# Attention scores by query blocks of one head, two heads in the two row halves of TensorE, in an attention, routing and expert kernel

## Chip, cores and metric

The kernel runs on one core of a Trainium2 chip. The metric is the device time of one launch in microseconds (us). A core has five engines that run side by side and meet only through semaphores: TensorE (PE: matrix products and transposes; its weight loads are shown as PEld), VectorE (DVE), ScalarE (ACT), GpSimd (POOL) and SyncE (SP, which issues DMAs). SBUF is the working memory, of 128 partitions; PSUM holds what PE writes, in 8 banks of 512 fp32 columns. PE's clock has two levels, 2.4 and 1.2 GHz; a granted clock of 1.0 is the upper one.

## The reference

Three stages, each fed by the one before. Only the first is touched by the change.

```python
B, H, S, D = 4, 8, 576, 64                      # attention
scores = scale * np.matmul(q, k.transpose(0, 1, 3, 2))
scores = np.where(causal, -1e9, scores)
scores = scores - scores.max(-1, keepdims=True)
a = np.exp(scores); a /= a.sum(-1, keepdims=True) + 1e-09
local = np.matmul(a, v)
q_p = phi(q)                                     # where(q > 0, q, exp(q) - 1) + 1
mem_out = (q_p @ M_prev) / ((q_p * z_prev).sum(-1) + 1e-6)
x = g * mem_out + (1 - g) * local                # g = sigmoid(beta), per head
# then: a top-1 mixture of 8 experts over 2304 tokens, and a gated layer 512 -> 1536 -> 512
```

## The kernel before

`attention_moe_gated` builds three stages: `Attention.run` (with `Routing` planned into it), `Experts.experts`, `Experts.gated`. The change lies in `Attention` and in one piece of `Routing.logits`.

**Tiles.** Two heads make a pair `pi`, 16 pairs in all; two pairs make a load group `gi`. `turn` transposes q, k and phi(q) of a pair on PE, so that one head lies on partitions 0 to 63 and the other on 64 to 127. The scores are made with fp32r products, which keep fewer bits: q and k are split into a high and a low part (`q_part`, `k_part`; ACT writes the high one, DVE subtracts it for the low one), and a score is the sum of three products. A score block (`scores`, L345) has 64 query rows of each head, 128 rows in all. Its weights `qz` are block diagonal: the 64 rows of the one head meet zeros in the half of the other, so that one product with 128 contraction rows gives both heads. A pair has nine such blocks of 64 to 576 key columns.

**Softmax.** `masked` (DVE, L365) adds the causal mask and takes the row minimum of the negated scores out of PSUM; `exp` (ACT, L375) makes the exponents and their row sums; `turn_probs` (PE, L410) transposes them in pieces of 128 columns; `keep_probs` (ACT or DVE, L283 or L285) copies them into `pt`, with a copy of its own for a last piece of 64 rows. `out_part` (PE, L440) multiplies with v, the two heads in the two column halves of the array; `mem_part` (L426) adds the memory term.

**The factors.** After the nine blocks of a pair, `recip` (DVE, L384 and L385) takes the reciprocals of the 128x9 sums. `spread` (L390, POOL or DVE) multiplies them into a 128x576 diagonal pattern `dg`, `fan` (PE, L398) spreads `dg` over the partitions with two fp32 products of 288 columns, `fan_copy` keeps them as `rb`, and `out_scale` (DVE, L450) multiplies the output with `rb`.

**POOL.** Beside this POOL makes phi(q), once per load group: `phi_sum` (L258, L260, L262, L264) is four operations on 128x1152 values that follow each other, below called a phi chain; then DVE reduces (`phi_norm`) and POOL scales (`phi_scale`, L276).

**What sets the order.** `Plan` is a list scheduler that runs when the program is built. Each step has a rank, a cost for each engine that may take it, what it needs and what buffer it takes; `order` picks the step that can start first by these costs, and all engines' queues are written in that order. At run time each engine works strictly through its queue. Buffers are pools: three PSUM banks for scores, three for transposes, two for outputs.

Of the kernel before, what the change touches and what calls it, by code (L numbers as in the profile page):

```python
# [30 lines left out]
SMB = 4  # L31
# [9 lines left out]
ORDER = (8, 0, 7, 1, 6, 2, 5, 3, 4)  # L41
# [83 lines left out]
class Attention:  # L125


    def __init__(self, ctx, tc, q, k, v, M_prev, z_prev, beta, ident, routing, high):
# [7 lines left out]
        self.ps_s = ctx.enter_context(tc.tile_pool(name="ps_s", bufs=3, space=PSUM))  # L136
        self.ps_t = ctx.enter_context(tc.tile_pool(name="ps_t", bufs=3, space=PSUM))
        self.ps_o = ctx.enter_context(tc.tile_pool(name="ps_o", bufs=2, space=PSUM))
        self.constants(beta)

    def constants(self, beta):
# [26 lines left out]
        self.iog = cp.tile([P, H // 2], F32, name="iog")  # L168
        for j in range(2):
            r = slice(j * 64, (j + 1) * 64)  # L170
            nc.vector.tensor_copy(self.iog[r], og[r].rearrange("p (a j) -> p a j", j=2)[:, :, j])
        nc.vector.reciprocal(self.iog, self.iog)

        self.rows = cp.tile([P, 64], F32, name="rows64")
        nc.vector.tensor_tensor(self.rows, self.ident[:, 0:64], self.ident[:, 64:128], ALU.add)
        self.same = cp.tile([P, P], F32, name="same")
        nc.gpsimd.memset(self.same, 0.0)
        for j in range(2):
            r = slice(j * 64, (j + 1) * 64)
            nc.gpsimd.memset(self.same[r, r], 1.0)  # L180
# [151 lines left out]

    @staticmethod
    def spans(t):
        n = 64 * (t + 1)
        return [(0, n)] if n <= 512 else [(0, 288), (288, 576)]

    def scores(self, u, si):
        nc, (pi, n_) = self.nc, divmod(u, NQ)
        t = ORDER[n_]  # L340
        k0, k1 = self.spans(t)[si]
        z, kz = self.qz[pi % 2], self.kz[pi]
        self.Sp[u, si] = Sp = self.ps_s.tile([P, 512], F32, name="Sp", tag="Sp")
        for p_, (a, c) in enumerate(((0, 0), (0, 1), (1, 0))):
            nc.tensor.matmul(  # L345
                Sp[:, 0 : k1 - k0], lhsT=z[:, a, t, :], rhs=kz[:, c, k0:k1], start=(p_ == 0), stop=(p_ == 2)
            )

    def masked(self, u, si):

        pi, n_ = divmod(u, NQ)
        t = ORDER[n_]
        n = 64 * (t + 1)
        if n_ == 0:
            self.sums[pi] = self.w2.tile([P, NQ], F32, name="sums", tag="sums")
        if si == 0:

            o = 0 if n_ % 2 == 0 else self.two[u // NQ, n_ // 2][1]
            if n_ % 2 == 0:
                self.two[pi, n_ // 2] = self.sp.tile([P, 640], F32, name="Sm", tag="Sm", bufs=SMB), n  # L360
            self.Sm[u] = self.two[pi, n_ // 2][0][:, o : o + n]
            self.mx[u] = self.sp.tile([P, 2], F32, name="mx", tag="mx")
        k0, k1 = self.spans(t)[si]
        mx = self.mx[u]
        self.nc.vector.tensor_tensor_reduce(  # L365
            out=self.Sm[u][:, k0:k1], in0=self.Sp[u, si][:, 0 : k1 - k0],
            in1=self.mask[:, 512 - 64 * t + k0 : 512 - 64 * t + k1],
            scale=-0.125, scalar=3.0e38 if si == 0 else mx[:, 0:1],
            op0=ALU.add, op1=ALU.min, accum_out=mx[:, si : si + 1],
        )  # L370

    def exp(self, u):
        pi, n_ = divmod(u, NQ)
        si = len(self.spans(ORDER[n_])) - 1
        self.nc.scalar.activation(  # L375
            self.Sm[u], self.Sm[u], AF.Exp, scale=-1.0, bias=self.mx[u][:, si : si + 1],
            accum_out=self.sums[pi][:, ORDER[n_] : ORDER[n_] + 1],
        )

    def recip(self, pi):  # L380

        nc, hp = self.nc, pi % (H // 2)
        self.rc[pi] = rc = self.sp.tile([P, NQ], F32, name="rc", tag="rc", bufs=2)
        nc.vector.tensor_scalar(rc, self.sums[pi], 1e-9, self.iog[:, hp : hp + 1], ALU.add, ALU.mult)  # L384
        nc.vector.reciprocal(rc, rc)  # L385

    def spread(self, eng, pi):

        self.dg[pi] = dg = self.w2.tile([P, NQ, 64], F32, name="dg", tag="dg", bufs=1)
        (self.nc.vector if eng == "DV" else self.nc.gpsimd).tensor_tensor(  # L390
            dg, self.rows[:, None, :].to_broadcast([P, NQ, 64]), self.rc[pi][:, :, None].to_broadcast([P, NQ, 64]), ALU.mult
        )

    def fan(self, pi, bk):

        self.TR[pi, bk] = T = self.ps_t.tile([P, 512], F32, name="T", tag="T")
        dg = self.dg[pi].rearrange("p t r -> p (t r)")
        self.nc.tensor.matmul(T[:, :288], lhsT=self.same, rhs=dg[:, bk * 288 : (bk + 1) * 288], start=True, stop=True)  # L398
# [6 lines left out]
    def turn_probs(self, u, chunks):
        nc, t = self.nc, ORDER[u % NQ]
        self.TP[u, chunks[0]] = T = self.ps_t.tile([P, 512], F32, name="T", tag="T")
        for n, i in enumerate(chunks):
            kr = min(128, 64 * (t + 1) - 128 * i)
            nc.tensor.transpose(T[:kr, n * 128 : (n + 1) * 128], self.Sm[u][:, i * 128 : i * 128 + kr], self.ident)  # L410

    def keep_probs(self, eng, u, c0, c1, first):

        pi, t = u // NQ, ORDER[u % NQ]
        kr = min(128, 64 * (t + 1) - 128 * c0)
# [1269 lines left out]
```

## Time and profile before

| | us |
|---|---|
| timed runs | 1131.64, 1125.78, 1129.64; median 1129.64 |
| profiled execution, its own time | 1123.5 |
| its span (first to last instruction) | 1121.7, mean granted clock 0.97 |
| PE / PEld / DVE / ACT / POOL busy over the span | 1037.1 / 900.6 / 545.5 / 466.5 / 293.8 |
| attention: first score product to the copy of the last logits | 9.71 to 299.0 |

Attention with its routing is about the first quarter of the span; the experts and the gated layer, whose rows are nearly all PE, follow and are not touched. A busy PE is not a PE at its peak, since the recorded length of a product holds its latency; what a product costs in a stream is the distance to the start of the next one. Where rows are merged (x3), the first start and the count are shown, and the start of the next row tells how long they held the engine.

### The profile page before, as it was taken

Reading aid. Unit: us, or ns where it says so; the run is one execution under the profiler, and the core shown is the slowest. Engines: PE = TensorE matmul, PEld = TensorE weight load, DVE = VectorE, ACT = ScalarE, POOL = GpSimd, SP = SyncE. Lnnn points to the kernel's source line nnn. Section 1 sums busy time; section 2 is a strip of 40 time slices with the busy share of each in tenths; the row PEclk is TensorE's granted clock in tenths of the full one; section 3 lists DMA queues with packets and bytes.
Section 4 is the critical chain, followed back from the end, with each engine's and each line's share of the span. In section 5 each row is a group of like instructions: output and inputs, shape, how many; then the busy total and the mean of one; then the engine's idle time right before and its main releaser. Section 6 shows DMA issues by size and latency. Waiting matters only on the chain. (4 is left out here: it accounts for less than half of the span.)

```text
span 1121.7 us, 16871 instructions
## 1 busy us (share of the span) xinstructions
PE 1037.1 (92%) x6133; PEld 900.6 (80%) x6133; DVE 545.5 (49%) x1232; ACT 466.5 (42%) x1074; POOL 293.8 (26%) x287
## 2 busy tenths in 40 slices
PE   6998998999869799979987679999999999999997
PEld 5766776777559689968976579999899999999996
DVE  6888867767585153227225699941212111121112
ACT  5875776777545252126214365521212211221211
POOL 7667245333265152025114300000110100100101
PEclk9999999999979999989998989999999999999999
DMA  5646433322268264128224466500010100100000
GB/s 119 140 103 175 83 85 85 97 61 58 66 196 291 75 210 159 38 72 280 87 62 137 141 188 197 177 12 1 29 57 1 47 10 1 58 1 1 29 1 29
DMA packets 111899, 102.50 MB, mean 91 GB/s; under 512 B 69520, under 2 KB 86928, under 8 KB 111760
## 3 DMA queue, kind: packets, MB, share of 16 engines
q1 hardware_dynamic: 107888, 88.18, 26.8%
q0 software_dynamic: 3872, 12.62, 3.7%
q8 instruction: 69, 1.13, 0.5%
q14 instruction: 70, 0.57, 0.2%
HBM read 84.49 MB, written 16.28 MB: 90 GB/s over the span
## 5 line engine op out<-in xcount | busy, mean ns | idle before, releaser
L1482 DVE TENSOR_TENSOR G<-G,pT 128x384 f32<-128x384 f32 (+1 forms) x74 | 40.1, 543 | 248.7 <-PE pT L1468 248.5
L1514 POOL DMA_INDIRECT out_dram<-o,rows x18 | 17.5, 971 | 462.7 <-ACT o L1510 213.5
L345 PE MATMUL Sp<-kz,qz 128*128 128x288 f32 (+8 forms) x480 | 100.3, 340 | 7.6 <-DVE mx L365 7.6
L1489 ACT ACTIVATE Gh<-G 128x384 fp32r<-128x384 f32 (+1 forms) x74 | 38.2, 516 | 162.3 <-DVE G L1482 162.1
L1478 ACT ACTIVATE G<-pH 128x384 f32<-128x384 f32 x72 | 35.4, 491 | 129.9 <-PE pH L1468 129.8
L345 PEld LDWEIGHTS Sp<-kz,qz 128*128 128x128 f32 x480 | 73.9, 197 | 17.0 <-DVE mx L365 9.5
L375 ACT ACTIVATE Sm<-Sm,mx 128x576 f32<-128x576 f32 (+2 forms) x144 | 79.8, 557 | 16.3 <-DVE mx L365 16.0
L1102 POOL TENSOR_TENSOR W<-raw,W 128x1024 fp32r<-128x1024 f32 x23 | 60.5, 2632 | 76.5 <-ACT W L1097 76.4
L365 DVE CUSTOM_DVE_ANT_0 Sm<-Sp,mask 128x288 f32<-128x288 f32 (+2 forms) x144 | 63.4, 450 | 18.8 <-PE Sp L345 12.4
L1499 PE MATMUL pX<-W,Gh 128*128 128x512 f32 x220 | 68.9, 394 | 0.0
L1097 ACT ACTIVATE W<-raw 128x1024 fp32r<-128x1024 f32 x60 | 61.7, 1054 | 16.9 <-DMA y_dram<-y 8.4
L283 ACT ACTIVATE pt<-T 64x128 f32<-64x128 f32 (+4 forms) x159 | 53.6, 368 | 31.9 <-PE T L410 28.2
L410 PE MATMUL T<-ident,Sm 128*128 128x128 f32 (+1 forms) x400 | 61.6, 281 | 5.0 <-ACT pt L283 3.4
L440 PE MATMUL O<-pt,vn 128*64 128x288 f32 (+4 forms) x512 | 59.5, 352 | 0.0
L1102 DVE TENSOR_TENSOR W<-raw,W 128x1024 fp32r<-128x1024 f32 x37 | 55.0, 1497 | 7.1 <-ACT W L1097 7.1
L1487 DVE TENSOR_TENSOR Gl<-G,Gh 128x384 fp32r<-128x384 f32 (+1 forms) x74 | 40.4, 546 | 33.9 <-ACT Gh L1489 33.9
L410 PEld LDWEIGHTS T<-ident,Sm 128*128 128x128 f32 (+1 forms) x400 | 43.3, 136 | 16.5 <-ACT pt L283 5.1
L1233 PE MATMUL pH<-W,xh 128*128 128x512 f32 x80 | 28.4, 501 | 28.3 <-issue 28.1
L1468 PE MATMUL pT<-xh,W 128*128 128x384 f32 x264 | 52.5, 342 | 0.0
L1468 PE MATMUL pT<-yh,W 128*128 128x384 f32 x264 | 51.3, 336 | 0.0
L440 PEld LDWEIGHTS O<-pt,vn 128*64 128x64 f32 (+1 forms) x512 | 30.4, 137 | 23.6 <-issue 11.2
L1468 PE MATMUL pH<-yh,W 128*128 128x384 f32 x240 | 46.9, 337 | 1.4 <-DVE xl L1457 1.4
(325 smaller groups left out, 2459.5 us busy)
## 6 DMA issues: line engine op xcount, KB each, us to landing
raw<-in_moe_w_dram SPq DMA_DIRECT2D x60, 512.0 KB, 4.9
raw<-in_moe_w_gate_dram SPq DMA_DIRECT2D x12, 512.0 KB, 4.3
raw<-in_moe_w_val_dram SPq DMA_DIRECT2D x12, 512.0 KB, 3.7
raw<-in_moe_w_out_dram SPq DMA_DIRECT2D x12, 512.0 KB, 3.3
y_dram<-y SPq DMA_DIRECT2D x9, 513.0 KB, 3.1
qn<-in_q_dram SPq DMA_DIRECT2D x32, 128.0 KB, 2.8
kn<-in_k_dram SPq DMA_DIRECT2D x32, 128.0 KB, 2.7
zf<-in_z_prev_dram SPq DMA_DIRECT2D x32, 128.0 KB, 5.8
```

Of the source, the lines that this page charges most:

```text
L283: self.nc.scalar.activation(out, in_, AF.Copy)
L345: nc.tensor.matmul(Sp[:, 0 : k1 - k0], lhsT=z[:, a, t, :], rhs=kz[:, c, k0:k1], start=(p_ == 0), stop=(p_ == 2))
L365: self.nc.vector.tensor_tensor_reduce(out=self.Sm[u][:, k0:k1], in0=self.Sp[u, si][:, 0 : k1 - k0], in1=self.mask[:, 512 - 64 * t + k0 : 5 ...
L375: self.nc.scalar.activation(self.Sm[u], self.Sm[u], AF.Exp, scale=-1.0, bias=self.mx[u][:, si : si + 1], accum_out=self.sums[pi][:, ORDER[ ...
L410: nc.tensor.transpose(T[:kr, n * 128 : (n + 1) * 128], self.Sm[u][:, i * 128 : i * 128 + kr], self.ident)
L440: nc.tensor.matmul(O[j * 64 : (j + 1) * 64, q0 - q0b : 288], lhsT=self.G[gi, "v"][:kr, i, 2 * l + j, :], rhs=PT[:kr, j, i, q0:q1], start=( ...
L1097: self.nc.scalar.activation(hi, t, AF.Copy)
L1102: eng.tensor_tensor(lo, t, hi.bitcast(F32), ALU.subtract)
L1468: nc.tensor.matmul(t, lhsT=w[:, k * P : (k + 1) * P], rhs=x[:, k, :], start=(m == k == 0), stop=(m == 2 and k == 3),)
L1482: nc.vector.tensor_tensor(t, t, p, ALU.mult)
L1487: nc.vector.tensor_tensor(l, t, hi.bitcast(F32), ALU.subtract)
L1499: nc.tensor.matmul(po[g][jj], lhsT=a[:, ts], rhs=w, start=(f == 0 and m == 0), stop=(f == NF - 1 and m == 2), skip_group_check=True,)
```

## The change

**Scores.** The blocks of 64 query rows of both heads become blocks of 128 query rows of one head (128 x 128, 256, 384 or 512 keys). The contraction is then 64 rows: head 0 uses the upper half of PE's rows and head 1 the lower, as tiles of 64x128, and their products alternate in the queue, into two PSUM banks of one buffer. Rows 512 to 575 stay as they were, one block-diagonal block of 576 columns (`z8`). There are still nine mask steps with ten instructions, nine exponents and 25 transposes in a pair, with 3136 instead of 2880 score columns; the copies out of the transposes are 10 instead of 13. `q_part` works on all 128 partitions at once, with four small pieces for `z8`.

**Factors.** `recip` becomes four DVE instructions on 128x9 values, which end in a high and a low part side by side (128x18). PE transposes these (`rc_turn`), a copy keeps them (18x128), and `fan` spreads them with six fp32r products against a constant choice matrix `pick` (made once on POOL). `spread` is gone.

**Buffers.** Scores: two buffers of two banks; transposes and outputs share four banks. Output halves are 384 and 192 columns instead of twice 288.

```diff
-ORDER = (8, 0, 7, 1, 6, 2, 5, 3, 4)
+ORDER = (3, 0, 2, 1, 4)
...
-        self.ps_s = ctx.enter_context(tc.tile_pool(name="ps_s", bufs=3, space=PSUM))
-        self.ps_t = ctx.enter_context(tc.tile_pool(name="ps_t", bufs=3, space=PSUM))
-        self.ps_o = ctx.enter_context(tc.tile_pool(name="ps_o", bufs=2, space=PSUM))
+        self.ps_s = ctx.enter_context(tc.tile_pool(name="ps_s", bufs=2, space=PSUM))
+        self.ps_t = ctx.enter_context(tc.tile_pool(name="ps_t", bufs=4, space=PSUM))
...
+    PARTS = ((0, 0), (0, 1), (1, 0))
...
+    def scores(self, pi, c):
+        nc, kz = self.nc, self.kz[pi]
+        self.Sp[pi, c] = Sp = self.ps_s.tile([P, 2, 512], F32, name="Sp", tag="Sp")
+        if c < 4:
+            n, q = 128 * (c + 1), self.qT[pi % 2]
+            for p_, (a, k) in enumerate(self.PARTS):
+                for j in range(2):
+                    r = slice(j * 64, j * 64 + 64)
+                    nc.tensor.matmul(
+                        Sp[:, j, 0:n], lhsT=q[r, a, c * 128 : (c + 1) * 128], rhs=kz[r, k, 0:n],
+                        start=(p_ == 0), stop=(p_ == 2), skip_group_check=True,
+                    )
+        else:
+            for i, (k0, k1) in enumerate(self.spans(8)):
+                for p_, (a, k) in enumerate(self.PARTS):
+                    nc.tensor.matmul(
+                        Sp[:, i, 0 : k1 - k0], lhsT=self.z8[pi % 2][:, a, :], rhs=kz[:, k, k0:k1],
+                        start=(p_ == 0), stop=(p_ == 2),
+                    )
...
-        self.rc[pi] = rc = self.sp.tile([P, NQ], F32, name="rc", tag="rc", bufs=2)
-        nc.vector.tensor_scalar(rc, self.sums[pi], 1e-9, self.iog[:, hp : hp + 1], ALU.add, ALU.mult)
-        nc.vector.reciprocal(rc, rc)
-
-    def spread(self, eng, pi):
-
-        self.dg[pi] = dg = self.w2.tile([P, NQ, 64], F32, name="dg", tag="dg", bufs=1)
-        (self.nc.vector if eng == "DV" else self.nc.gpsimd).tensor_tensor(
-            dg, self.rows[:, None, :].to_broadcast([P, NQ, 64]), self.rc[pi][:, :, None].to_broadcast([P, NQ, 64]), ALU.mult
-        )
+        self.rc[pi] = rc = self.sp.tile([P, 2 * NQ], F32, name="rc", tag="rc", bufs=2)
+        t = self.sp.tile([P, NQ], F32, name="rs", tag="rs", bufs=2)
+        nc.vector.scalar_tensor_tensor(t, self.sums[pi], 1e-9, self.iog[:, hp], ALU.add, ALU.mult)
+        nc.vector.reciprocal(t, t)
+        nc.vector.tensor_copy(rc.bitcast(F32R)[:, 0:NQ], t)
+        nc.vector.tensor_tensor(rc[:, NQ:], t, rc[:, 0:NQ], ALU.subtract)
+
+    def rc_turn(self, pi):
+        self.TR[pi] = T = self.ps_t.tile([P, 512], F32, name="T", tag="T")
+        self.nc.tensor.transpose(T[0 : 2 * NQ, 0:P], self.rc[pi], self.ident)
...
-        dg = self.dg[pi].rearrange("p t r -> p (t r)")
-        self.nc.tensor.matmul(T[:, :288], lhsT=self.same, rhs=dg[:, bk * 288 : (bk + 1) * 288], start=True, stop=True)
+        r = self.rT[pi]
+        for n in range(3) if bk == 0 else (3,):
+            o = (n - 3 * bk) * P
+            self.nc.tensor.matmul(T[:, o : o + P], lhsT=self.pick[:, n], rhs=r, start=True, stop=True, skip_group_check=True)
+        for j in range(2 * bk):
+            self.nc.tensor.matmul(
+                T[:, P : P + 64], lhsT=self.pick[:, 4 + j], rhs=r[:, j * 64 : (j + 1) * 64],
+                start=(j == 0), stop=(j == 1), skip_group_check=True,
+            )
```

On PE, a stretch of the second pair before: each row `L345` is three products with 128 contraction rows, and a block of 64 rows of both heads.

```order
L345 MATMUL Sp<-kz,qz_107 128x512 x3
L295 MATMUL T<-ident,qn 128x128 x4
L299 MATMUL T<-ident,qn 128x64
L410 MATMUL T<-ident,Sm 128x128 x2
L345 MATMUL Sp<-kz,qz_107 128x128 x3
L345 MATMUL Sp<-kz,qz_107 128x448 x3
L345 MATMUL Sp<-kz,qz_107 128x192 x3
```

The same place now: `L373` is the score product of a half (six: three parts for each of two heads), `L455` the transposes of exponents, `L311` and `L315` those of q and k, `L380` the last block.

```order
L373 MATMUL Sp<-kz,qT_105 128x512 x6
L455 MATMUL T<-ident,Sm 128x128 x7
L373 MATMUL Sp<-kz,qT_105 128x128 x6
L311 MATMUL T<-ident,qn 128x128 x4
L315 MATMUL T<-ident,qn 128x64
L455 MATMUL T<-ident,Sm 64x128
L455 MATMUL T<-ident,Sm 128x128 x4
L373 MATMUL Sp<-kz,qT_105 128x384 x6
L373 MATMUL Sp<-kz,qT_105 128x256 x6
```

The score groups are fewer and twice as long in count, and each now stands as 64x128 tiles between transposes that use the whole array.

On PE, where the factors of the last pair are spread, before (`L398` is `fan`, `L440` is `out_part`, `L426` is `mem_part`):

```order
L398 MATMUL T<-dg,same 128x288
L440 MATMUL O<-pt_144,vn 64x288 x2
L440 MATMUL O<-pt_144,vn 64x160 x2
L440 MATMUL O<-pt_144,vn 64x32 x2
L398 MATMUL T<-dg,same 128x288
L426 MATMUL O<-phT,MB 128x288
```

and now (`L427` is `rc_turn`, `L439` and `L441` are `fan`, `L489` is `out_part`):

```order
L427 MATMUL T<-ident,rc 18x128
L489 MATMUL O<-pt_147,vn 64x384 x2
L439 MATMUL T<-rT,pick 128x128 x4
L441 MATMUL T<-rT,pick 128x64 x2
L489 MATMUL O<-pt_147,vn 64x256 x2
L489 MATMUL O<-pt_147,vn 64x128 x2
L475 MATMUL O<-phT,MB 128x384
```

A transposition stands ahead, and the two fp32 products of 288 columns have become six small ones.

On DVE, the end of the first pair before (`L384` and `L385` are `recip`; `L310` the low part of q, `L365` masks):

```order
L384 TENSOR_SCALAR rc<-sums,iog 128x9
L385 RECIPROCAL rc<-rc 128x9
L310 TENSOR_TENSOR qz_106<-T,qz_106 64x6x64 x2
L310 TENSOR_TENSOR qz_106<-T,qz_106 64x3x64 x2
L365 ISA Sm,mx<-Sp,mask 128x128
```

and now, at the end of the second pair (`L402` masks, `L346` the low part of k, `L301` copies):

```order
L402 ISA Sm,mx<-Sp,mask 128x128
L402 ISA mx 128x1
L346 TENSOR_TENSOR kz<-T,kz 128x192
L420 SCALAR_TENSOR_TENSOR rs<-sums,iog 128x9
L421 RECIPROCAL rs<-rs 128x9
L422 CAST rc<-rs 128x9
L423 TENSOR_TENSOR rc<-rs,rc 128x9
L301 COPY pt_147<-T 128x2x128
L402 ISA Sm,mx<-Sp,mask 128x384
```

Four instructions that read and write SBUF alone stand where two stood, and masks and copies queue behind them.

## Rows read from the trace of the kernel before

**Rows 1.** Windows: stretch, length, busy us of PE, PEld, DVE, ACT, POOL; clock; DMA.
```profile
10.00:130.00 120.00, 108.40 (x723) 82.91 (x722) 98.37 (x284) 83.82 (x256) 77.19 (x54) 0.97 0.57 132
130.00:290.00 160.00, 156.06 (x1124) 118.75 (x1122) 111.97 (x373) 117.02 (x358) 62.24 (x48) 0.99 0.29 71
```

**Rows 2.** Timeline of PE (start, length): score products (L345) and what starts next.
```profile
135.25 0.39 PE L345 MATMUL Sp<-kz,qz 128*128 128x512 f32 x1
135.48 0.27 PE L410 MATMUL T<-ident,Sm 128*128 128x128 f32 x1
...
136.09 0.39 PE L345 MATMUL Sp<-kz,qz 128*128 128x128 f32 x2
136.31 0.30 PE L410 MATMUL T<-ident,Sm 128*128 128x128 f32 x1
```

**Rows 3.** Timeline of PE: outputs (L440, two column halves) and a memory product (L426, whole array).
```profile
139.78 1.44 PE L440 MATMUL O<-pt,vn 128*64 128x288 f32 x10
...
143.38 0.41 PE L426 MATMUL O<-phT,MB 128*128 128x288 f32 x1
143.62 0.71 PE L410 MATMUL T<-ident,Sm 128*128 128x128 f32 x5
```

**Rows 4.** Timeline of PE: a 64-row transpose (L299) between products on the whole array.
```profile
144.16 0.49 PE L295 MATMUL T<-ident,ph 128*128 128x128 f32 x3
...
144.49 0.27 PE L295 MATMUL T<-ident,ph 128*128 128x128 f32 x1
144.69 0.27 PE L299 MATMUL T<-ident,ph 64*128 64x64 f32 x1
144.90 0.41 PE L345 MATMUL Sp<-kz,qz 128*128 128x320 f32 x1
```

**Rows 5.** DVE by line and shape, 10 to 290 us: busy us, mean ns.
```profile
L310 DVE TENSOR_TENSOR qz<-T,qz 64x384 fp32r<-64x384 f32 x30 | 16.6, 553 | 3.0 <-ACT qz L312 2.6
L310 DVE TENSOR_TENSOR qz<-T,qz 64x192 fp32r<-64x192 f32 x30 | 10.6, 352 | 1.6 <-ACT qz L312 1.3
L384 DVE TENSOR_SCALAR rc<-sums,iog 128x9 f32<-128x9 f32 x16 | 8.7, 542 | 0.6 <-ACT Sm L375 0.5
L390 DVE TENSOR_TENSOR dg<-rows,rc 128x576 f32<-128x576 f32 x2 | 6.4, 3221 | 0.0
```

**Rows 6.** Timeline of POOL and DVE: small DVE work while POOL works.
```profile
39.38 3.12 POOL L260 TENSOR_SCALAR e<-e 128x1152 f32<-128x1152 f32 x1
39.49 3.04 DVE L384 TENSOR_SCALAR rc<-sums,iog 128x9 f32<-128x9 f32 x1
42.56 0.22 DVE L385 RECIPROCAL rc<-rc 128x9 f32<-128x9 f32 x1
42.58 2.63 POOL L262 TENSOR_TENSOR ph<-ph,e 128x1152 f32<-128x1152 f32 x1
...
183.22 2.54 DVE L828 TENSOR_TENSOR r_d<-L,r_mx 128x40 f32<-128x40 f32 x1
185.68 0.20 DVE L832 TENSOR_TENSOR r_sel<-O,L 128x40 f32<-128x40 f32 x1
...
306.61 2.52 POOL L1102 TENSOR_TENSOR W<-raw,W 128x1024 fp32r<-128x1024 f32 x1
...
306.84 2.33 DVE L915 CAST ranki<-rank 128x18 int32<-128x18 f32 x1
```

**Rows 7.** Windows around two such stretches, and behind each (columns as in rows 1).
```profile
107.00:113.00 6.00, 3.07 (x23) 2.54 (x22) 5.91 (x7) 1.85 (x6) 5.85 (x3) 1.00 0.39 151
113.00:117.00 4.00, 2.95 (x17) 2.30 (x18) 3.88 (x12) 2.31 (x6) 2.63 (x1) 0.72 0.00 0
...
180.00:186.00 6.00, 3.00 (x21) 2.09 (x19) 5.90 (x7) 1.27 (x6) 5.84 (x3) 1.00 0.13 46
186.00:189.00 3.00, 2.43 (x10) 2.33 (x11) 2.93 (x10) 1.93 (x7) 2.41 (x1) 0.58 0.23 87
```

More of the change, by code (lines that the diff above doesn't have):

```diff
@@ L30 @@
 NT = NTOK // P
-SMB = 4
+SMB = 5
+QB = ((0, 384), (384, 576))
 WARM1 = 18
@@ L166, in constants @@
         nc.vector.tensor_scalar(og, g, -1.0, 1.0, ALU.mult, ALU.add)
-        self.iog = cp.tile([P, H // 2], F32, name="iog")
+        nc.vector.reciprocal(og, og)
+        self.iog = cp.tile([P, H // 2, NQ], F32, name="iog")
+        o2 = og.rearrange("p (a j) -> p a j", j=2)
+        for c in range(4):
+            nc.vector.tensor_copy(self.iog[:, :, 2 * c : 2 * c + 2], o2)
         for j in range(2):
             r = slice(j * 64, (j + 1) * 64)
[L171 to L180, printed above, removed]
+            nc.vector.tensor_copy(self.iog[r, :, 8:9], o2[r, :, j : j + 1])
         self.gf = cp.tile([P, 2, 18], F32, name="gf")
@@ L355, in masked @@
+    def masked(self, pi, n, si):
+        c, j = divmod(n, 2)
+        w = self.spans(n)[-1][1]
+        if n == 6:
             self.sums[pi] = self.w2.tile([P, NQ], F32, name="sums", tag="sums")
         if si == 0:
[L358 to L362, printed above, removed]
@@ L363, in masked @@
-        k0, k1 = self.spans(t)[si]
-        mx = self.mx[u]
+            two = pi, min(c, 3 - c), j
+            o = 0 if c > 1 else 128 * (4 - c)
+            if c > 1:
+                self.two[two] = self.sp.tile([P, 640], F32, name="Sm", tag="Sm", bufs=SMB)
+            self.Sm[pi, n] = self.two[two][:, o : o + w]
+            self.mx[pi, n] = self.sp.tile([P, 2], F32, name="mx", tag="mx")
+        k0, k1 = self.spans(n)[si]
+        mx = self.mx[pi, n]
+        mask = self.mask[:, 384 - 128 * c :] if n < 8 else self.mask8 if si else self.mask[:, 0:288]
@@ L405, in turn_probs @@
[L405 to L415, printed above, removed]
-        T = self.TP[u, first]
+        r = self.rT[pi]
@@ new lines, in turn_probs, with keep_probs @@
+    def turn_probs(self, pi, n, chunks):
+        nc = self.nc
+        self.TP[pi, n, chunks[0]] = T = self.ps_t.tile([P, 512], F32, name="T", tag="T")
+        for o, i in enumerate(chunks):
+            kr = chunk_rows(i)
+            nc.tensor.transpose(T[:kr, o * 128 : (o + 1) * 128], self.Sm[pi, n][:, i * 128 : i * 128 + kr], self.ident)
+    def keep_probs(self, eng, pi, n, chunks):
+        i0, w = chunks[0], len(chunks)
+        pt, T = self.pt[pi % 2], self.TP[pi, n, i0]
+        c, j = divmod(n, 2)
+        if n < 8:
+            self.copy(eng, pt[:, j, 0:w, c * 128 : (c + 1) * 128], T[:, : w * 128].rearrange("p (i q) -> p i q", q=128))
+            return
+        kr = chunk_rows(i0)
@@ L469, in run @@
         add("cp", -1000, {"PL": 3}, lambda e: None)
+        add("pick", 6, {"PL": 4}, lambda e: self.choices())
         def ac(n):
@@ L501, in run @@
             gi, u0 = pi // 2, pi * NQ
-            before = [("S", u, si) for u in range(u0 - 2 * NQ, u0 - NQ) if u >= 0 for si in range(len(self.spans(ORDER[u % NQ])))]
+            before = [("S", pi - 2, c) for c in ORDER] if pi > 1 else []
             for g in range(2):
@@ L559, in run @@
             r = u0 + 20
-            add(("r", pi), r, {"DV": 0.5}, lambda e, a=pi: self.recip(a), needs=[("e", u0 + n_) for n_ in range(NQ)],
+            add(("r", pi), r, {"DV": 0.7}, lambda e, a=pi: self.recip(a), needs=[("e", pi, n) for n in range(NQ)],
                 takes=[("rc", pi)], uses=[("sums", pi)])
-            add(("D", pi), r, {"PL": 1.6, "DV": 0.75}, lambda e, a=pi: self.spread(e, a), needs=[("r", pi)], takes=[("dg", pi)], uses=[("rc", pi)])
+            add(("rt", pi), r, {"PE": 0.15}, lambda e, a=pi: self.rc_turn(a), needs=[("r", pi)], takes=[("T", ("rt", pi))], uses=[("rc", pi)])
@@ L574, in run @@
                     needs = [("o", pi, bk, i - 1)] if i else [("L", "v", gi)]
-                    needs += [k for t in range(9) if t >= 2 * i and (t <= 4 if bk == 0 else t >= 4) for k in kept[t]]
-                    n = 288 - max(0, i * 128 - bk * 288)
+                    needs += [k for n in range(NQ) if n // 2 >= i and (n < 6) == (bk == 0) for k in kept[n]]
+                    n = QB[bk][1] - max(QB[bk][0], i * 128)
                     add(("o", pi, bk, i), r, {"PE": PO + n * 4 / 2400}, lambda e, a=(pi, bk, i): self.out_part(*a), needs=needs,
-                        takes=[] if i else [("O", (pi, bk))], uses=[("vn", gi)] + ([("O", (pi, bk))] if i else []))
```

243 lines of the change are left out of this document (131 added, 112 removed).

## The prediction

> **What bounds the kernel now.** I read the windows first, to see which engine is full in attention. From 130 to 290 us PE is busy 156.06 of 160 us, DVE and ACT 111.97 and 117.02; from 10 to 130 us PE has 108.40 of 120, DVE 98.37 [rows 1]. A busy PE need not be dense, so I next read PE's timeline. There products follow each other at their own spacing for microseconds on end, and work taken off PE shortens the second stretch nearly one for one. In the first stretch DVE is close behind, and part of it is no work: small DVE instructions that wait for POOL [rows 6]. So the change has two sides: what it takes off PE, and what it does to that waiting.
>
> **PE, scores.** Spacing comes from starts. A 512-column product holds PE for 0.23 us (135.25 to 135.48), a 128-column one for 0.11 (two from 136.09 to 136.31) [rows 2]. In proportion to 512, 256 columns cost 0.115 and 384 0.172; I take 0.12 and 0.175 (320: 0.146, 448: 0.205), and 0.11 as the floor below. A pair before had three products each of 64, 128, 192, 256, 320, 384, 448 and 512 columns: 3 x (0.11 x 3 + 0.12 + 0.146 + 0.175 + 0.205 + 0.23) = 3.62 us. The block of 576 stands on both sides and drops out. Now there are three products for each head with 128, 256, 384 and 512 columns. If the two heads run beside each other, a couple costs what one costs: 3 x (0.11 + 0.12 + 0.175 + 0.23) = 1.91 us. If they don't: 3.81.
>
> No row shows two row halves at once. The nearest are the column halves of `out_part`: ten recorded products of 288 columns start between 139.78 and 140.81, five couples at about 0.24 us, and one on the whole array takes the same 0.24 (143.38 to 143.62) [rows 3]. The second head is free there. I take that for rows too, and keep 3.81 as the other end. The gain is 1.71 us a pair, 27.4 us in 16 pairs (at the other end a loss of 3.0).
>
> **PE, changes of tile shape.** A whole-array transpose is followed by the next after 0.11 us (three between 144.16 and 144.49); into a 64-row tile it takes 0.20 (144.49 to 144.69), and out of it 0.21 (to 144.90) [rows 4]. So a change of shape costs about 0.09 us each way. In the order I count 230 changes in attention before and 345 now, leaving out the transposes with 64 output rows, around which the timeline shows no such step. 115 x 0.09 = 10.4 us lost. The Trainium skill ("TensorEngine Tiling (Array Packing)", Key Properties) has the rule behind it: changing the tiling mode, not just the tile, drains TensorE. The trace agrees, at 0.09 us; without that rule the sum would be some 7 us better.
>
> **PE, factors.** `fan` before is two fp32 products of 288 columns, each in two recorded halves of 0.24 like the memory product of rows 3: 0.97 us a pair. Now one transpose and six small products at the 0.11 floor: 0.78. Gain 0.2, or 3 us in all.
>
> PE together: 27.4 + 3.0 - 10.4 = 20 us less to do. How much of it shows? The second stretch holds 9.3 of the 16 pairs (160 of 275 us) and passes most of it, I take 85%; the first is shared with DVE, I take half. 20 x (9.3 x 0.85 + 6.7 x 0.5) / 16 = 14 us.
>
> **DVE and ACT, work.** The low part of q goes from 2 x 553 + 2 x 352 = 1.81 us to about 1.3 a pair [rows 5], and ACT's high part alike; three copies of thirteen go; 256 more score columns a pair take about 0.27 back on each; the two `spread`s that fell to DVE go (6.4 us) [rows 5]. A few tenths of a microsecond a pair, on engines that are not the bound: no time of its own, and what lets PE's gain through. The new constants (`pick`, fourteen small POOL instructions) take the place of larger memsets on the same engine, ahead of the first phi chain: nothing, I estimate, within 1 us either way.
>
> **DVE, waiting for POOL.** This speaks against the change. `recip` at 39.49 took 3.04 us and ended with POOL's L260, the reciprocal behind it 0.22 while L262 ran; a cast of 128x18 took 2.33 beside POOL's L1102 [rows 6]. So a scalar operation, a cast and a product of two SBUF tensors wait until POOL's instruction ends; a reciprocal doesn't. Before, the 16 `recip` starts took 8.7 us instead of 16 x 0.22, 5.2 us of waiting, and the two `spread`s 6.4 [rows 5]: 11.6 in all. Now three of four instructions can wait. The first catches the rest of a POOL instruction (1.5 us of 3.1), then POOL starts the next of its chain at once (42.58 behind 42.50) and the cast waits for all of that (2.7). The last slips in behind: at 185.68 a second product took 0.20 right after one that had waited 2.54 [rows 6].
>
> How often? I counted masks and exponents ahead of each `phi_exp` on ACT and each `recip` on DVE in the new order. Of 16 `recip`s, numbers 1, 4, 8 and 12 stand about 0.3 pair behind the start of a phi chain, which lasts 0.7 pair: inside. Numbers 3, 6 and 10 stand beside `phi_scale`. 4 x 4.2 + 3 x 1.5 = 21 us, 10 more than before. PE loses half of such time: 3.07 of 6 us busy in one such stretch, 3.00 of 6 in another, and then its clock falls (0.72 over 4 us, 0.58 over 3), 1.2 us each [rows 7]. 10 x 0.5 + 1.2 = 6 us.
>
> The Trainium skill ("SBUF — State Buffer", Who interferes with whom) says that DVE and GpSimd share a port pair as an exclusive lock: copies, casts and tensor_scalar can take it, and two SBUF inputs meet GpSimd's reads. The trace agrees for each kind. By the rule alone the last subtraction waits too: 4 x 6.9 + 4.5 = 32 us, and 11 us lost instead of 6; the row at 185.68 makes me leave it out.
>
> **Sum.** -14 + 6 = -8 us. On the profiled execution (1123.5, span 1121.7) that is 1115.5. The median of the timed runs is 1129.64, 6.1 above it, and I take the same 8 us off that: 1121.6.
>
> **Rivals.**
> 1. The two row halves don't overlap, and the change doesn't do what it says. PE then has 3.0 more for scores, 10.4 for shapes, 3.0 less for factors: +10; with +6 of waiting, 1145.6. For it: no row shows row halves together. Against: rows 3. Chance 0.08.
> 2. `recip` against the phi chain decides, and the kernel becomes slower. The place is DVE's queue at a pair's end: masks and copies stand behind the waiting `recip`, PE waits for them, and `rc_turn` stands in PE's queue itself. If all eight phi chains are met and all three instructions wait: 8 x 6.9 = 55 us, 43 more than before, half of it on PE, 22, and four more falls of the clock, 5: +27 - 14 = +13, 1142.6. It decides from 28 us of extra waiting. For it: rows 6 and 7. Against: in the timeline five of 16 met a POOL instruction before, and the mean of 542 ns is far from a full wait each [rows 5]. Chance 0.10.
> 3. PE is not what ends the waits. Scores, mask, exponent, transpose, copy are a chain per block, and transposes and outputs now share four banks instead of three and two; PE's gain becomes waiting for a bank or a mask. 5 of the 14 us remain and 6 go: +1, 1130.6. For it: DVE at 82% in the first stretch. Against: PE's density in the second. Chance 0.22.
> 4. All of PE's 20 us pass and the waits for POOL stay as they are: 1109.6. Chance 0.14.
>
> **How the numbers follow.** The forecast has 0.46, with its own range 1114 to 1127. Measurement tells about 0.5% from no change, 5.6 us. Faster: 0.36 of the forecast's 0.46, all of rival 4, 0.02 of rival 3: 0.52. Same: 0.10 of the forecast, 0.17 of rival 3, 0.01 of rival 2: 0.28. Slower: 0.20. The range for 8 in 10 reaches to rival 4 with a few us to spare, for waits that vanish, and past rival 2: 1104 to 1143; most of rival 1 is left out.
>
> **What would show it.** Right: score products of the two heads start within 0.01 us of each other, couples at 0.11 to 0.23; DVE's cast beside a phi instruction takes 2 to 3 us in three to six pairs; attention's last logits copy about 8 us earlier. Wrong: couples at twice that spacing (rival 1); casts at 0.2 throughout (rival 4) or long ones in all chains, with PE idle behind them and a lower clock (rival 2); PE idle ahead of transposes or scores, released by copies and masks (rival 3). A gain in the experts or the gated layer would be none of these.

## The result, and the profile after

Four runs of the changed kernel took 1140.93 to 1142.84 us, median 1141.67, beside 1127.71 for the kernel before in the same session: **slower by 1.33%**, ratio 1.0133 (95% interval 1.0092 to 1.0173). The forecast was 1121.6. The profiled execution is the one of 1142.84 us, span 1140.9, mean granted clock 0.952 instead of 0.970. Nearly all of the loss lies in attention: its last logits copy ends at 315.5 us instead of 299.0. What follows takes 825.4 us instead of 822.7; the same code takes 816 to 831 in the profiled executions below.

The windows of the changed kernel, columns as in [rows 1]:

```profile
10.00:130.00 120.00, 99.90 (x681) 70.44 (x683) 90.82 (x277) 76.96 (x238) 70.76 (x53) 0.89 0.65 132
130.00:290.00 160.00, 146.50 (x1081) 102.62 (x1081) 120.59 (x378) 105.05 (x322) 49.64 (x31) 0.94 0.28 71
```

PE is busy for 246 of 280 us instead of 264, and the granted clock is 0.89 and 0.94 instead of 0.97 and 0.99. PE did become less loaded, but the time went up: it waits, and runs at the lower clock behind the waits.

The row halves do what the change says. PE's timeline, to set beside [rows 2]: six products of 384 columns, three for each head.

```profile
111.64 0.80 PE L373 MATMUL Sp<-kz,qT 64*128 64x384 f32 x6
112.36 0.33 PE L311 MATMUL T<-ident,ph 128*128 128x128 f32 x1
```

The next product starts 0.72 us after the first of the six. One after the other they would take 6 x 0.172 = 1.03; in couples 3 x 0.172 and a change of shape make 0.6 to 0.7. In the trace the two heads' products start 3 to 5 ns apart.

DVE by line and shape, 10 to 310 us (busy us, mean ns), beside [rows 5]:

```profile
L420 DVE SCALAR_TENSOR_TENSOR rs<-sums,iog 128x9 f32<-128x9 f32 x16 | 11.7, 732 | 0.0
L422 DVE CAST rc<-rs 128x9 fp32r<-128x9 f32 x16 | 10.7, 668 | 0.6
L346 DVE TENSOR_TENSOR kz<-T,kz 128x384 fp32r<-128x384 f32 x15 | 8.3, 556 | 4.0 <-ACT kz L350 3.9
L325 DVE TENSOR_TENSOR qT<-T,qT 128x384 fp32r<-128x384 f32 x15 | 8.2, 549 | 0.4 <-ACT qT L327 0.4
...
L423 DVE TENSOR_TENSOR rc<-rs,rc 128x9 f32<-128x9 f32 x16 | 5.0, 312 | 0.5
...
L421 DVE RECIPROCAL rs<-rs 128x9 f32<-128x9 f32 x16 | 3.4, 216 | 0.6
```

Four instructions on nine columns take 30.8 us in 16 pairs. Undisturbed ones take 0.17 to 0.22 each, about 12 in all, so nearly 19 us is waiting for POOL. The timeline of one such place (POOL, DVE; start and length), beside [rows 6]:

```profile
39.18 3.13 POOL L274 TENSOR_SCALAR ph<-qn 128x1152 f32<-128x1152 f32 x1
39.32 2.78 DVE L420 SCALAR_TENSOR_TENSOR rs<-sums,iog 128x9 f32<-128x9 f32 x1
...
42.14 0.21 DVE L421 RECIPROCAL rs<-rs 128x9 f32<-128x9 f32 x1
42.28 3.12 POOL L276 TENSOR_SCALAR e<-e 128x1152 f32<-128x1152 f32 x1
42.38 3.05 DVE L422 CAST rc<-rs 128x9 fp32r<-128x9 f32 x1
45.47 0.17 DVE L423 TENSOR_TENSOR rc<-rs,rc 128x9 f32<-128x9 f32 x1
```

The first instruction waits for the rest of L274, the reciprocal slips in, the cast waits for all of L276, the subtraction slips in, just ahead of POOL's next instruction at 45.49: as forecast. The largest holes in PE's work are elsewhere, though, in DVE's small **routing** instructions (L865 to L907), which the change does not touch:

```profile
116.09 3.12 POOL L276 TENSOR_SCALAR e<-e 128x1152 f32<-128x1152 f32 x1
...
116.40 2.63 DVE L869 TENSOR_TENSOR O<-r_t,r_vm 128x32 fp32r<-128x32 f32 x1
...
119.42 0.55 DVE L402 CUSTOM_DVE_ANT_0 Sm<-Sp,mask 128x384 f32<-128x384 f32 x1
...
119.89 0.42 DVE L402 CUSTOM_DVE_ANT_0 Sm<-Sp,mask 128x256 f32<-128x256 f32 x1
...
121.98 2.61 POOL L280 TENSOR_TENSOR e<-ph,zf 128x1152 f32<-128x1152 f32 x1
122.03 2.57 DVE L903 TENSOR_TENSOR sid<-sid,r_a 128x4 f32<-128x4 f32 x1
...
124.74 0.53 DVE L402 CUSTOM_DVE_ANT_0 Sm<-Sp,mask 128x384 f32<-128x384 f32 x1
```

The mask at 124.74 stands behind them in DVE's queue, and PE's next scores wait for its bank. The two masks between the waits (119.42, 119.89) are for one head each of two blocks; a buffer of two banks comes free only with the second head's mask, so PE stood still through both waits. In the kernel before, the one mask between two such waits freed a bank, and PE went on behind it (timeline, DVE and PE):

```profile
107.39 2.64 DVE L812 TENSOR_TENSOR O<-r_t,r_vm 128x32 fp32r<-128x32 f32 x1
...
109.93 0.41 DVE L365 CUSTOM_DVE_ANT_0 Sm<-Sp,mask 128x256 f32<-128x256 f32 x1
...
110.37 2.61 DVE L832 TENSOR_TENSOR r_sel<-O,L 128x32 f32<-128x32 f32 x1
110.40 0.66 PE L345 MATMUL Sp<-kz,qz 128*128 128x288 f32 x3 [0.99 <-DVE mx L365]
```

The windows around this place, in the changed kernel, and the second one like it, and behind each, beside [rows 7]:

```profile
117.60:125.40 7.80, 0.33 (x4) 0.07 (x1) 7.66 (x16) 2.57 (x10) 6.83 (x3) 0.63 0.26 68
125.40:130.00 4.60, 4.60 (x19) 3.17 (x21) 0.92 (x4) 1.38 (x5) 0.00 (x0) 0.52 0.68 182
197.20:203.50 6.30, 0.35 (x3) 0.11 (x3) 6.17 (x15) 2.39 (x8) 5.45 (x3) 0.84 0.32 71
203.50:208.30 4.80, 4.80 (x24) 3.93 (x24) 2.42 (x10) 2.81 (x8) 0.00 (x0) 0.50 0.36 110
```

In [rows 7] PE still did half its work while DVE waited in routing. Now it does none for 7.5 and 6.0 us, and then works for 4 to 5 us at a granted clock of 0.5, the lower level of 1.2 GHz. PE's waits by releaser show it (line waiting, line waited for: us, times, longest), first the kernel before from 20 to 296 us, then the changed one from 20 to 312:

```profile
PE Sp L345 <- DVE mx L365: 7.6, 4, 3.0
PE T L410 <- ACT pt L283: 3.4, 2, 2.2
PE T L295 <- DVE pt L285: 1.3, 1, 1.3
```

```profile
PE Sp L380 <- DVE mx L402: 7.5, 1, 7.5
PE T L311 <- DVE xT L505: 6.1, 3, 2.2
PE T L455 <- DVE xt L301: 6.0, 1, 6.0
PE T L311 <- DVE pt L301: 3.8, 1, 3.8
```

For an account of PE I took every distance between two starts, from 20 us to the end of attention. Up to the first quartile of its kind of succession at full clock I call it own work; the rest is waiting, or is set apart if it lies in a stretch at the lower clock. In us, and beside it DVE's waits for POOL (what an instruction takes beyond the shortest of its kind, where that is over 0.4 us) and stretches at the lower clock from 9 us on:

| kernel | own | waiting | extra at low clock | low clock | DVE waits: factors | routing |
|---|---|---|---|---|---|---|
| before | 236.6 | 37.7 | 4.7 | 3, 10.2 us | 5.0, and 4.7 in two `spread`s | 12.7 |
| after | 222.1 | 54.4 | 18.8 | 8, 47.6 us | 18.8 | 13.3 |

PE's own work fell by 14.5 us; waiting took 16.7 and the lower clock 14.1: +16.3, the 16.5 us by which attention ends later. The sum is fixed by the traces, the split is less so: with other ways of forming the kinds, own work falls by 8 to 24 us.

### The profile page after: what moved, and what is told of

Its sections match the earlier page's. It is cut to its first block, busy times and chain, and to the rows that moved or that the text cites. A ratio compares the mean times of both kernels' runs of the same rounds, so it can differ in the third digit from the quotient of the medians.

```text
span 1140.9 us, 16928 instructions
## 1 busy us (share of the span) xinstructions
PE 1039.0 (91%) x6181; PEld 886.2 (78%) x6181; DVE 547.2 (48%) x1266; ACT 457.2 (40%) x1049; POOL 275.0 (24%) x268
## 3 DMA queue, kind: packets, MB, share of 16 engines
q8 instruction: 70, 1.15, 0.5%
## 5 line engine op out<-in xcount | busy, mean ns | idle before, releaser
L410 ACT ACTIVATE Sm<-Sm,mx 128x512 f32<-128x512 f32 (+3 forms) x144 | 83.2, 579 | 31.0 <-DVE mx L402 30.6
L402 DVE CUSTOM_DVE_ANT_0 Sm<-Sp,mask 128x512 f32<-128x512 f32 (+3 forms) x144 | 65.1, 482 | 25.1 <-PE T L455 13.1
L455 PE MATMUL T<-ident,Sm 128*128 128x128 f32 (+1 forms) x400 | 66.1, 304 | 11.1 <-DVE xt L301 6.0
L1154 ACT ACTIVATE W<-raw 128x1024 fp32r<-128x1024 f32 x60 | 61.7, 1054 | 16.7 <-DMA y_dram<-y 7.9
L455 PEld LDWEIGHTS T<-ident,Sm 128*128 128x128 f32 (+1 forms) x400 | 47.7, 151 | 24.1 <-DVE xt L301 6.2
L299 ACT ACTIVATE pt<-T 128x512 f32<-128x512 f32 (+4 forms) x128 | 49.9, 434 | 32.3 <-PE T L455 31.2
L489 PE MATMUL O<-pt,vn 128*64 128x192 f32 (+4 forms) x512 | 60.6, 357 | 0.0
L373 PE MATMUL Sp<-kz,qT 64*128 64x512 f32 (+3 forms) x384 | 52.0, 382 | 2.0 <-DVE kz L346 1.3
L489 PEld LDWEIGHTS O<-pt,vn 128*64 128x64 f32 (+1 forms) x512 | 31.0, 139 | 23.1 <-issue 16.2
L1525 PEld LDWEIGHTS pT<-xh,W 128*128 128x128 f32 x264 | 47.4, 192 | 0.7
```

What stands on the lines that cost most here:

```text
L299: self.nc.scalar.activation(out, in_, AF.Copy)
L373: nc.tensor.matmul(Sp[:, j, 0:n], lhsT=q[r, a, c * 128 : (c + 1) * 128], rhs=kz[r, k, 0:n], start=(p_ == 0), stop=(p_ == 2), skip_group_ch ...
L402: self.nc.vector.tensor_tensor_reduce(out=self.Sm[pi, n][:, k0:k1], in0=self.Sp[pi, c][:, j if n < 8 else si, 0 : k1 - k0], in1=mask, scal ...
L410: self.nc.scalar.activation(self.Sm[pi, n], self.Sm[pi, n], AF.Exp, scale=-1.0, bias=self.mx[pi, n][:, si : si + 1], accum_out=self.sums[p ...
L455: nc.tensor.transpose(T[:kr, o * 128 : (o + 1) * 128], self.Sm[pi, n][:, i * 128 : i * 128 + kr], self.ident)
L489: nc.tensor.matmul(O[j * 64 : (j + 1) * 64, q0 - q0b : q1 - q0b], lhsT=self.G[gi, "v"][:kr, i, 2 * l + j, :], rhs=PT[:kr, j, i, q0:q1], st ...
```

## Experiments

Times are compared as ratios to the kernel before, run on the same chip beside them. One per cent is 11.3 us.

**POOL's instructions cut, changed kernel.** Nothing moves on PE, DVE and ACT; each of POOL's five phi instructions, `phi_scale` among them, becomes six of 192 elements:

```diff
-            nc.gpsimd.tensor_scalar(ph, q, 0.0, None, ALU.max)
+        for c in range(0, 18 * 64, 18 * 64 // PIECES):
+            v = slice(c, c + 18 * 64 // PIECES)
...
+                nc.gpsimd.tensor_scalar(ph[:, v], q[:, v], 0.0, None, ALU.max)
```

> The changed kernel with each of POOL's five phi instructions cut into six of 192 elements; the order on every other engine is the same. Theory A (what the change lost, it lost where small DVE instructions wait for POOL's phi instructions, in the reciprocals and, newly, in the routing steps that the new order puts beside them, with PE idle behind and at the lower clock): no DVE instruction then waits over 0.7 us for POOL, the PE gaps of 7.5, 6.0 and 3.8 us shrink below 2, at most three falls of the clock remain before 315 us instead of eight, and the time is 1118 to 1128. Theory B (products on half the rows don't keep PE's clock up): the waits shrink, but six or more falls remain and the time is 1135 or more. Theory C (two double score buffers and four shared banks make PE wait for masks and copies): the gaps of PE stay where they are with other releasers, time 1135 to 1142.

Measured 1116.08, ratio 0.9875 (0.9845 to 0.9905): 2.6% below the changed kernel from this edit alone. Routing now runs in the midst of POOL's pieces (timeline, POOL and DVE):

```profile
112.68 2.64 POOL L278 TENSOR_SCALAR ph<-qn 128x192 f32<-128x192 f32 x4
114.20 0.22 DVE L876 TENSOR_TENSOR O<-r_t,r_vm 128x32 fp32r<-128x32 f32 x1
115.29 3.29 POOL L280 TENSOR_SCALAR e<-e 128x192 f32<-128x192 f32 x5
116.49 0.17 DVE L908 TENSOR_SCALAR r_a<-r_a 128x4 f32<-128x4 f32 x1
116.99 0.16 DVE L910 TENSOR_TENSOR sid<-sid,r_a 128x4 f32<-128x4 f32 x1
```

What took 2.63, 1.48 and 2.57 us takes 0.22, 0.17 and 0.16; DVE's waits fall from 32.1 to 6.4 us, the three low-clock stretches left are 34.2 us instead of 47.6 in eight. Theory A holds as to the cause, though its time (1118 to 1128) was at least 2 us too high; theory B's six falls and 1135 are out. Two points of A failed: one long wait remains, the longest of all, and around its end PE is idle for 3.8 us.

```profile
47.28 3.34 POOL L282 TENSOR_TENSOR ph<-ph,e 128x192 f32<-128x192 f32 x6
48.28 5.64 DVE L427 SCALAR_TENSOR_TENSOR rs<-sums,iog 128x9 f32<-128x9 f32 x1
50.58 3.32 POOL L284 TENSOR_TENSOR e<-ph,zf 128x192 f32<-128x192 f32 x6
53.96 0.22 DVE L428 RECIPROCAL rs<-rs 128x9 f32<-128x9 f32 x1
```

**The same cut, kernel before.**

> The kernel before with the same cut of POOL's phi instructions. Theory A: its 15 us of DVE waiting for POOL and its three falls of the clock go as well, but there is less to get back: 3 to 8 us, 1120 to 1125, so that the changed kernel with the cut is level or up to 5 us ahead of it. Theories B and C: 0 to 8 us here, and the changed kernel with the cut stays 10 us or more behind it.

1119.03, ratio 0.9904 (0.9875 to 0.9934): A again, with more to get back than its 3 to 8 us. The waits for POOL cost the kernel before about 0.96%, 10.8 us, and the changed one 2.6%.

**One reciprocal.** The factors' split into high and low part moves behind the transpose, where its input is PSUM:

```diff
-        nc.vector.scalar_tensor_tensor(t, self.sums[pi], 1e-9, self.iog[:, hp], ALU.add, ALU.mult)
-        nc.vector.reciprocal(t, t)
-        nc.vector.tensor_copy(rc.bitcast(F32R)[:, 0:NQ], t)
-        nc.vector.tensor_tensor(rc[:, NQ:], t, rc[:, 0:NQ], ALU.subtract)
+        nc.vector.reciprocal(rc, self.sums[pi])
...
+            self.nc.vector.tensor_tensor(self.rT[LO : LO + NQ], t, self.rT.bitcast(F32)[0:NQ], ALU.subtract)
```

> The changed kernel with DVE's four instructions of the factors cut to one reciprocal (the kind that did not wait for POOL): the split into high and low part is made behind the transpose, from PSUM, and 1 - g is multiplied in by the copy of the spread factors. The order changes in some 300 rows of PE and DVE. Theory A: the waits of the reciprocals (16.5 us of the 32) go, those of the routing stay unless the order moves them; 1129 to 1136. Theories B and C: within 3 us of the changed kernel, 1139 to 1145.

1131.88, ratio 1.0020 (0.9997 to 1.0044): the factors' 18.8 us of waiting are gone for 1.1%, some 13 us. Routing is as it was:

```profile
109.57 2.64 DVE L873 TENSOR_TENSOR O<-r_t,r_vm 128x32 fp32r<-128x32 f32 x1
...
113.63 1.48 DVE L905 TENSOR_SCALAR r_a<-r_a 128x4 f32<-128x4 f32 x1
...
115.21 2.57 DVE L907 TENSOR_TENSOR sid<-sid,r_a 128x4 f32<-128x4 f32 x1
```

**Both edits.**

> Both edits together, the cut phi instructions and the single reciprocal. Theory A: 1116 to 1127, about level with the cut alone, since both take away the same waiting at the reciprocals; DVE has three instructions fewer a pair. Theories B and C: 1135 or more.

1117.69, ratio 0.9905 (0.9884 to 0.9926). No wait for POOL's phi instructions is left in the factors or in routing. From the single reciprocal to this one 1.15%, 13 us, for routing's 13.2 us of waiting. So freed of POOL the change is level with the old structure (0.9905 and 0.9904, uncertain by 0.36%; 0.9875 with the cut alone). The profiled executions, one of each, are less kind to it: attention ends at 298.2 us with the cut alone, 293.0 with both edits and 290.2 in the old kernel with the cut, and what follows takes 822, 821 and 831. What became of PE's 14.5 us?

**Banks.** The old scores with the change's PSUM (four and four); the new ones with three single banks for scores and five shared, with before's three, three and two, and with four singles:

```diff
-        self.ps_s = ctx.enter_context(tc.tile_pool(name="ps_s", bufs=3, space=PSUM))
-        self.ps_t = ctx.enter_context(tc.tile_pool(name="ps_t", bufs=3, space=PSUM))
-        self.ps_o = ctx.enter_context(tc.tile_pool(name="ps_o", bufs=2, space=PSUM))
+        self.ps_s = ctx.enter_context(tc.tile_pool(name="ps_s", bufs=4, space=PSUM))
+        self.ps_t = ctx.enter_context(tc.tile_pool(name="ps_t", bufs=4, space=PSUM))
```

> The kernel before with POOL's phi instructions cut, and PSUM dealt out as in the changed kernel: four banks for scores, four for transposes and outputs together, in place of three, three and two. Theory C1 (with the waits for POOL gone, the change's gain on PE is lost because outputs hold two of the four shared banks while transposes wait for them): 3 to 8 us slower than the cut kernel before (1119.0), 1122 to 1127, PE's waits ahead of transposes and outputs up by that. Rival C2 (the gain is lost in the chain of mask, exponent, transpose and copy, which now comes for two heads at once, whatever the banks): within 2 us of 1119, 1117 to 1121.

> The changed kernel with the cut phi instructions and the single reciprocal (1117.7 us), with scores in three single banks, of which a block of two heads takes two, and five banks for transposes and outputs; an output waits until its factors are spread, and a transpose of factors until the last ones are used. Theory C1: a fifth bank takes away waits ahead of transposes: 1108 to 1115. Rival C2: scores now wait for masks as well, 1118 to 1126.

> As the run with three and five banks, but with PSUM as in the kernel before: three banks for scores, three for transposes, two for outputs. Theory C1: outputs no longer hold transposes up, 1110 to 1116. Rival C2: 1118 to 1126, as with three and five.

> The same kernel (1117.7 us) with four banks for scores and four shared ones, as in the change, but each head's scores in a bank of their own, free as soon as that head is masked. Theories C1 and C2 alike: little, 1114 to 1119, since PE's visible waits ahead of scores are only 2 us there. If scores' banks bound PE after all (masks late by a whole block), 1112 or less.

1124.02 (0.9945, 0.9909 to 0.9982), 1124.74 (0.9955, 0.9921 to 0.9989), 1116.16 (0.9866, 0.978 to 0.995) and 1118.18 (0.9895, 0.981 to 0.998). The first is 0.4% above the old kernel with the cut, the third 0.4% below the new one with both edits, both in C1's direction, but each within its uncertainty (0.5 and 0.9%). C1's gain from a fifth bank did not come; there PE's waits ahead of scores grew from 2.0 to 10.0 us. Banks alone settle nothing.

**One score product of three.** How much of PE's time shows?

```diff
-    PARTS = ((0, 0), (0, 1), (1, 0))
+    PARTS = ((0, 0),)
```

> The changed kernel with the cut phi instructions and the single reciprocal (1117.7 us), of whose three score products per block only the first is left (the two with the low parts are left out; their operands are still made), so that PE has about 1.8 us a pair less to do, 29 us in all, and nothing else moves. Theory P (PE still sets the pace of attention; 70 to 85 per cent of what it saves shows): 1093 to 1098. Theory L (in the changed kernel PE waits at so many places for masks, exponents and copies that less than half of its time shows): 1104 to 1118.

> The kernel before with the cut phi instructions (1119.0 us) and the same two products left out: about 3.0 us a pair, 48 us in all. Theory P: 1078 to 1086. Theory L, if it holds of the old scores too, with less than half showing: 1095 or more; if the old kernel passes most and the new one less than half, what the change saves beyond some 20 us is lost to the next engine in both.

> The changed kernel as it is (1141.7 us) with the two products left out, 29 us less on PE. Theory P: 1117 to 1122. Theory L: 1130 or more, with a lower clock, since the waits for POOL stay as long and PE has less to do beside them.

> The kernel before (1127.7 us) with the two products left out, 48 us less on PE. The prediction's own shares (85 per cent in the second stretch, half in the first) would make 34 us of it, 1094. Theory L: less than 24 us, 1104 or more.

The times: 1102.87 (0.9796, 0.9746 to 0.9847), 1099.21 (0.9727, 0.9701 to 0.9753), 1126.89 (1.0000, 0.9975 to 1.0025) and 1106.24 (0.9811, 0.9779 to 0.9843), that is 12.3, 20.0, 15.0 and 21.3 us less than the same kernel with three products. What that is a share of depends on the count. By the account above PE's own work fell by 16.7, 30.3, 14.4 and 29.7 us, and 74, 66, about 100 and 72 per cent of it shows, theory P's share. But a group of score products, from its first start to the start of what follows (median at full clock), got shorter by 27 to 28 us in all in the new blocks and by 42 in the old, close to the 29 and 48 expected; of this 45, 47, 53 and 50 per cent shows. Two of the times, 1099.21 and 1106.24, lie in theory L's ranges and none in P's. So about half of PE's time shows, or more, in both structures alike; the runs don't decide between P and L. They show no clearly smaller share in the new structure than in the old.

**Without factors.** The steps from `recip` to `fan_copy` left out, outputs multiplied by ones, the rest in the same order:

```diff
-            add(("r", pi), r, {"DV": 0.2}, lambda e, a=pi: self.recip(a), needs=[("e", pi, n) for n in range(NQ)],
+            add(("r", pi), r, {"DV": 0.2}, lambda e: None, needs=[("e", pi, n) for n in range(NQ)],
```

> The changed kernel with the cut phi instructions and the single reciprocal (1117.7 us), with its factors left out: no reciprocal, transpose, split, spreading products and their copies, outputs are multiplied by ones; all other instructions in the same order. PE has some 15 us less. Theory F (the chain of factors holds outputs, their banks and PE up, and that eats the change's gain): 1098 to 1104, at least 6 us below the old kernel without factors. Theory S (double score blocks and banks eat it): 1105 to 1111, within 4 us of the old kernel without factors.

> The kernel before with the cut phi instructions (1119.0 us), with its factors left out in the same way, 13 us less on PE. By the share of PE's time that showed (65 per cent): 1110 on either theory, 1107 to 1113; what tells them apart is the distance to the new kernel without factors.

> The kernel before with the cut phi instructions and PSUM dealt out as in the change (1124.0 us), without factors. If four shared banks cost only while outputs wait in them for their factors (part of theory F): within 2.5 us of the old kernel without factors. If they cost by themselves (theory S): 4 to 7 us above it.

1085.86 (0.9623, 0.9595 to 0.9652), 1077.73 (0.9549, 0.9524 to 0.9575) and 1075.29 (0.9537, 0.9507 to 0.9568). The values are others, tokens go to other experts, and the stage after attention, about 800 us, is 21 to 32 us shorter in all three, which the expectations had not reckoned with; only their distances count. Theory F is out: without factors the new scores are 0.74% (8 us) behind the old ones, with 13 us less own work on PE (209.3 and 222.4). The profiled executions don't show these 8 us: the new kernel's was the fastest of five, and attention ends at 277.8 us in it and at 279.1 in the old one's. Shared banks cost nothing there (-0.1%), so if they cost at all, it is while outputs wait in them for factors. PE's waits in the new kernel without factors (20 to 277 us), then in the old one (20 to 279):

```profile
PE Sp L388 <- DVE mx L410: 3.3, 2, 1.7
PE T L466 <- DVE z L344: 3.1, 1, 3.1
PE T L466 <- DVE xT L516: 1.9, 1, 1.9
PE T L466 <- DVE kz L354: 1.8, 2, 1.4
PE T L466 <- ACT xt L307: 1.7, 1, 1.7
```

```profile
PE T L302 <- ACT xt L290: 3.9, 1, 3.9
PE Sp L352 <- DVE mx L372: 3.3, 3, 1.9
PE T L417 <- ACT pt L290: 1.2, 1, 1.2
```

The new waits stand ahead of the transposes of probabilities (L466), released by copies that free a bank, not by exponents. I summed the time beyond 0.2 us ahead of these transposes where a DVE or ACT reader of a transpose or output bank had ended within 0.13 us: 13.5 us here against 1.9, 11.1 with both edits against 0.8, and 12.1 in the changed kernel against 5.7 before. Behind exponents it is 0.0 to 0.3 in each.

## Why the prediction was wrong, point by point

- **Scores side by side (27.4 us less): right in kind.** Rival 1 is out. Scores' own work went from 67.9 to 44.8 us, 23.1 less, with the changes of shape around them.
- **Changes of shape and factors (+10.4, -3.0).** They can't be told apart in the account. By the account PE's own work fell by 14.5 us instead of 20; factors, with their transpose, became dearer (12.9 to 15.2), since the small products change the shape at both ends.
- **"14 of the 20 us pass": failed.** Where score products alone were left out, 45 to 53 per cent of the time that they held PE showed, or 66 to 100 by the account, against my 70; but the change also brings waits of its own, and they ate what passes. Freed of POOL, the change gains 0.0 to 0.3%, not 14 us. That is rival 3 (0.22), and of its two candidates, a bank or a mask, it is the bank by the sums above (11.1 us against 0.8): copies behind the transposes come later. What holds those copies up, the masks and exponents of two heads at once or the order as such, is not shown; dealing the banks out otherwise did not settle it.
- **DVE and ACT's own work: no time.** No run speaks against it.
- **"DVE waits 10 us more": right, in part by luck.** 22.4 before (5.0, 4.7 and 12.7), 32.1 after: +9.7. Reciprocals 1, 4, 8 and 12 (from 0) were hit, as counted; 0 was hit too (1.4 us at 26.5), and 3, 6 and 10, beside `phi_scale`, were not. I read the row at 185.68 too far: that product started 0.1 us before POOL's next instruction, as the last subtraction did by 0.02 us at 45.47; at 90.45, with POOL's L278 running since 90.25, it waited 2.47 us, and at the other two places no POOL instruction followed. The Trainium skill ("SBUF — State Buffer", Who interferes with whom) has a DVE instruction with two SBUF inputs contend with a GpSimd instruction that reads SBUF, and whoever issues first keeps the port pair for its whole instruction. The trace agrees at these places; beside `tensor_scalar` pieces of 192 it does not (last section).
- **"Half on PE and one clock fall, +6": the step that failed most.** I gave the added 10 us the old price, and left routing's 12.7 us out, since they stand on both sides. But the price is not fixed, and instead of one more fall of the clock there were five, with 14.1 us of extra time instead of 1.2. The cut gave 10.8 us back in the kernel before, for the 18.0 us of waiting that went, 0.6 for each; in the changed one 29 for 25.7, or with both edits 25.7 for 32.1, 0.8 to 1.1 for each (the times are uncertain by 3 us in the old kernel and by 5 to 6 in the new). Routing's waits are as long as they were, but PE stands still for 7.5 and 6.0 us where it stood for 4.0 and 3.6, and each of the eight stretches at 1.2 GHz follows a hole of 1.6 us or more. That PE has less score work to put beside a wait is not the reason, as far as the runs tell: with two of three score products left out, POOL's waits cost 2.04% in the changed kernel (1.0000 against 0.9796; 2.28% with all products) and 0.84% in the kernel before (0.9811 against 0.9727; 0.96%), each uncertain by about half a per cent, and PE's holes at routing are 7.5 and 6.4 us in the one and 5.0 and 4.8 in the other. What the rows show is where the waits fall: at the first place neither two-bank buffer comes free between them, at the second PE's transposes stand behind DVE's copy `xt` (6.0 us). Whether the buffers or the order as such make the price is open, since neither was changed with POOL's instructions whole. That a new order and new buffers change what an old wait costs was in none of my terms.
- **Rival 2** gave nearly the time (1142.6), by luck: it needed 28 us more waiting at the reciprocals. There were 9, and routing made half of the price.

Together: of the forecast's -14 nothing to -3 us came, and its +6 became +15 to +18. With both edits the change is level and its waits for POOL cost 15 us more than before's (25.7 against 10.8); with the cut alone it is 3 us ahead and they cost 18 more. Either way 15 us, the 1.33%.

The best versions beat both kernels: the changed one with the cut alone (0.9875), and with both edits and before's banks (0.9866, uncertain by 0.9%), about 1.3% below the kernel before. The kernel before with the cut alone has most of that (0.9904).

## What to carry to other kernels

A wait on a side engine has no price of its own: it costs what the bounding engine can't cover, and a new order or new buffers change that for waits that were there already (routing's 13 us left PE idle for 7.6 us before and 13.4 after). So look up what stands behind each such wait in the new queues, and don't take its price over from the old ones. Look for long instructions of one engine that hold up short ones of another, and cut them before tuning what waits for both. After a change of tiling, see whether the transposes or the products now wait for a bank.

## What the runs showed of the hardware

- Short DVE instructions that waited 1.3 to 2.6 us beside POOL instructions of 1152 elements ran in 0.16 to 0.39 us in the midst of `tensor_scalar` pieces of 192, where I had expected waits of up to one piece.
- Beside back-to-back `tensor_tensor` pieces one DVE instruction waited through to the end of the chain, 5.64 us over 11 of them (and 4.17 over 8 in the kernel before with the cut). Others got in between such pieces in 0.2 to 0.5; what decides is open.
- A reciprocal of 128x9 never waited (0.22 us), which makes it the cheap form beside a busy POOL.
